# Head loads in modulation row pieces, three K blocks with their own history, and a new order of all engines, in a fused adaLN block on one Trainium2 core

## The chip, the core and the metric

The kernel runs on one core of a Trainium2 chip. The core has five instruction streams that run side by side and wait for each other through semaphores: TensorE (PE, matmuls), VectorE (DVE), ScalarE (ACT), GpSimd (POOL) and SyncE (SP, which here only issues DMAs). The metric is the device time of one execution in microseconds (us). All matrices are bf16.

## What is computed

One transformer block with modulation from a condition vector, for 2048 rows of 512 numbers. Cut to what matters:

```python
sa, ca, ga, sb, cb, gb = (silu(c) @ w_mod).reshape(6, 512)      # c: 1 x 512, w_mod: 512 x 3072
h = layernorm(x) * (1 + ca) + sa
q, k, v = h @ wqkv                                              # 32 heads of 16
# row s attends to the 8 rows s, s-2, ..., s-14 (rows before 0 are masked)
logits = einsum(q[s], k[s - 2w]) / 4;  attn = softmax(logits over w);  o = sum(attn * v[s - 2w])
x = x + ga * (o @ wo)
h = layernorm(x) * (1 + cb) + sb
x = x + gb * ((gelu(h @ w_gate) * (h @ w_up)) @ w_down)         # inner width 1792
```

## The kernel before, in words

**Groups.** The 2048 rows are worked in four groups of 512 (`sg` 0 to 3). A group goes through the first norm, its transposition to `hT` (columns on partitions), the projections to Q, K and V, the window attention, the output projection, the second norm and the feed-forward part. The four groups overlap: while one is in its feed-forward matmuls, the next ones are in attention.

**Attention.** Q, K and V lie transposed, in four column blocks `j`. For each block DVE multiplies Q with eight shifted views of K (`pq`, line 664, 128 x 4096 numbers), and PE sums the products over the 16 numbers of a head with a matrix of ones (`LTp`, line 678; small tiles, four side by side). After the softmax (mask, maximum, subtraction, exp, sum, reciprocal, probabilities: lines 690 to 722) DVE multiplies the probabilities with shifted copies of V (`pv`, line 771), and PE sums these over the window (`o_ps`, line 790). V's shifted copies come through memory: `vT` is stored (line 635) and loaded four times with different offsets into one tile `V` (line 644), each piece some 510 KB.

**K and its history.** `kT` (line 170) holds 16 columns and then three blocks of 512. Group `sg` writes block `sg % 3`, and its eight views reach back into the block before it, so a product of group 1 also waits for group 0's K. Group 3 takes block 0 again; one copy (`halo`, line 630) brings the last 16 columns of group 2 to the front for it.

**The head.** Group 0 is loaded in two halves of two 128-row chunks. Columns 0 to 1023 of `w_mod` (shift `sa` and scale `ca`) come as two DMAs of 512 columns each (`ldwm01`, line 242). PE multiplies each with silu(c): 16 small matmuls for one half (line 348), 16 for the other; DVE adds them up into `mod01` (line 355). Until there is work, PE runs 20 filler matmuls (`warmup`, line 217). Group 0's chunks are transposed on PE, two at a time (`th0`, `th1`; line 509), and evicted with scale and shift to `hT` by ACT (line 545) and DVE (line 543). The first two Q blocks are projected in halves of 256 rows as these come in (line 580), all else in 512 rows (line 598).

**The order.** Every step is an `Op` of a generator, with its engine; the list `ORDER` names, step by step, which generator goes on. So each engine's instruction order is fixed by hand, and an instruction that waits holds up all behind it on its engine. The names used below are those of the steps: `pq.1.3` is the product of group 1, block 3; `lp.1` group 1's last logits matmuls; `qp.1.0.2` the projection of group 1, Q (0; K is 1, V is 2), block 2; `pv.0.0` the first PV product and `o.0.2` the matmuls on the third; `mp2` to `mp5` the products for the other four modulation vectors, whose loads are `wm2` to `wm5`.

**Buffers.** PSUM is shared out as four banks `mm` (projections, feed-forward, modulation), two `att` (transposes, PV sums, output projection) and one tile `lg` of two banks for the logits. A matmul that needs a bank waits for the eviction of the one before in it. All big loads go through SP's queue, in the order of the list.

**The steps named in the prediction.** Normalisation: statistics on DVE (lines 430, 431) or ACT (408 to 419), reciprocal root on POOL (471), application on DVE (448). Groups 2 and 3 are transposed by a DMA (line 490); group 2's scale and shift is then done on POOL (line 525), group 3's on ACT (line 527).

Of the kernel before, what the change touches and what calls it, by code (L numbers as in the profile page):

```python
# [9 lines left out]
ALU = mybir.AluOpType  # L10
# [44 lines left out]
]  # L55


def _ap(base, free_dims):
    return bass.AP(base.tensor, base.offset, [list(base.ap[0])] + [list(d) for d in free_dims])


class Slots:


# [913 lines left out]
```

## Time and profile before

| what | value |
|---|---|
| time of three runs | 236.69 us median (236.52 to 236.73) |
| profiled execution: its span, from the first to the last instruction | 234.1 us |
| median of the runs less that span | 2.6 us |
| PE busy | 230.0 us, 98% of the span |
| DVE, ACT, POOL busy | 170.4, 150.0, 18.6 us |
| bytes moved | 30.21 MB, mean 129 GB/s |
| granted TensorE clock | 1.000 (mean of the span) |

The profiled execution's own time is known as its span; the runs are timed around it. A row of the timeline gives the start, the length, the engine, the line, the operation, what it writes and reads, and how many were merged into it. PEld is the loading of weights ahead of a matmul. A DMA row of SP is the issue alone; its landing is given in a view of its own, in us from the issue. The chain of work follows the end of the kernel back, from each step to what released it. In the view by stretch, an engine's busy time stands beside the length of the stretch.

### The profile page before, as it was taken

How to read it: one execution, taken by the hardware profiler on the slowest of the kernel's cores; microseconds unless marked ns; L12 is line 12 of the kernel's file. 1: busy time of each engine (PE TensorE's matmuls, PEld its weight loads, DVE VectorE, ACT ScalarE, POOL GpSimd, SP SyncE). 2: the span in 40 equal slices, each digit the busy share in tenths (PEclk: the TensorE clock that was granted, in tenths of full speed). 3: DMA queues.
4: the chain of work that ended last, by engine and by line, in shares of the span. 5: the costliest groups of instructions: out<-in, count | busy, mean ns of one | idle time of the engine just before them, and what ended most of it. 6: DMA issues, size and time to landing. Idle time of an engine off the chain costs nothing.

```text
span 234.1 us, 3675 instructions
## 1 busy us (share of the span) xinstructions
PE 230.0 (98%) x1387; PEld 108.2 (46%) x1387; DVE 170.4 (73%) x240; ACT 150.0 (64%) x283; POOL 18.6 (8%) x43
## 2 busy tenths in 40 slices
PE   7999999999999999999999999999999999999995
PEld 2755455434644444444444444444444444444443
DVE  3999999999997999999799788467747421222222
ACT  4899997976997758936656492546754343666400
POOL 2612461000100000100000010000001000000000
PEclk9999999999999999999999999999999999999999
DMA  6997989999969839553102963510000411000011
GB/s 218 373 364 213 202 213 171 276 391 303 176 152 236 291 92 200 98 114 103 56 0 57 202 109 60 156 56 0 0 4 0 90 45 45 3 0 0 0 48 45
DMA packets 36265, 30.21 MB, mean 129 GB/s; under 512 B 14872, under 2 KB 34328, under 8 KB 36248
## 3 DMA queue, kind: packets, MB, share of 16 engines
q1 hardware_dynamic: 35968, 29.72, 50.6%
q10 hardware_dynamic: 280, 0.26, 0.3%
q8 instruction: 11, 0.18, 0.3%
q14 instruction: 6, 0.05, 0.1%
HBM read 22.37 MB, written 4.98 MB: 117 GB/s over the span
## 4 chain that ended last, share of the span: by engine, by line
PE 98%; DVE 0%; issue 0%
PE g_ps L844 21%; PE u_ps L844 21%; PE y_ps L856 19%; PE qkv_ps L598 17%; PE x_ps L811 6%; PE o_ps L790 3%; PE LTp L678 3%; PE warm_ps L217 3%; PE y_ps L868 1%; PE qkv_ps L580 1%; PE hTp L484 1%; PE hTp L509 0%; PE modT_ps L305 0%; PE modT_ps L348 0%; PE gR_ps L369 0%; PE PTp L736 0%
## 5 line engine op out<-in xcount | busy, mean ns | idle before, releaser
L844 PE MATMUL g_ps<-h,Wg 128*128 128x512 bf16 x224 | 57.5, 379 | 0.0
L844 PE MATMUL u_ps<-h,Wu 128*128 128x512 bf16 x224 | 57.5, 379 | 0.0
L878 ACT ACTIVATE gl<-g_ps 128x512 bf16<-128x512 f32 x56 | 33.6, 600 | 24.8 <-PE g_ps L844 23.9
L856 PE MATMUL y_ps<-Wd,hht 128*128 128x512 bf16 x210 | 46.0, 379 | 0.0
L885 ACT CAST ub<-u_ps 128x512 bf16<-128x512 f32 x56 | 32.8, 586 | 18.3 <-PE u_ps L844 18.1
L598 PE MATMUL qkv_ps<-hT,wqkv 128*128 128x512 bf16 x184 | 42.1, 380 | 0.0
L896 DVE TENSOR_TENSOR hht<-gl,ub 128x512 bf16<-128x512 bf16 x56 | 23.0, 421 | 25.3 <-ACT ub L885 25.0
L664 DVE TENSOR_TENSOR pq<-qT,kT 128x4096 bf16<-128x4096 bf16 x16 | 36.3, 2292 | 0.0
L771 DVE TENSOR_TENSOR pv<-PT,V 128x4096 bf16<-128x4096 bf16 x16 | 36.0, 2286 | 0.0
L844 PEld LDWEIGHTS <-Wg 128*128 128x128 bf16 x224 | 21.5, 98 | 27.3 <-issue 2.1
L844 PEld LDWEIGHTS <-Wu 128*128 128x128 bf16 x224 | 21.8, 98 | 26.6 <-issue 0.4
L856 PEld LDWEIGHTS <-hht 128*128 128x128 bf16 x210 | 20.5, 98 | 24.8
L598 PEld LDWEIGHTS <-wqkv 128*128 128x128 bf16 x184 | 20.1, 114 | 19.7 <-issue 3.0
L903 DVE TENSOR_TENSOR ot<-y_ps,x 128x512 bf16<-128x512 f32 x15 | 10.3, 689 | 20.2 <-PE y_ps L856 17.2
L471 POOL TENSOR_TENSOR rstd<-rstd,neghalf 128x4 f32<-128x4 f32 (+1 forms) x9 | 8.8, 980 | 154.1 <-DVE rstd L460 85.5
L527 ACT ACTIVATE h<-h,modT,scl 128x512 bf16<-128x512 bf16 x12 | 8.8, 802 | 11.6 <-DMA h<-xn 11.6
L811 PE MATMUL x_ps<-woP,oT 128*128 128x512 bf16 x64 | 15.3, 379 | 0.0
L430 DVE BATCH_NORM_STATS2 st<-x 128x6 f32<-128x512 bf16 x19 | 12.9, 680 | 3.1 <-DMA x<-in_A_x_dram 2.9
L820 DVE TENSOR_TENSOR x<-x_ps,x 128x512 bf16<-128x512 f32 x16 | 10.8, 686 | 5.0 <-PE x_ps L811 5.0
L801 ACT CAST oT<-o_ps 128x512 bf16<-128x512 f32 x16 | 8.9, 592 | 2.7 <-PE o_ps L790 2.7
L618 ACT CAST qT<-qkv_ps 128x512 bf16<-128x512 f32 x16 | 9.2, 587 | 2.2 <-PE qkv_ps L598 2.1
L620 ACT CAST kT<-qkv_ps 128x512 bf16<-128x512 f32 x16 | 9.5, 596 | 1.2 <-PE qkv_ps L598 1.2
(85 smaller groups left out, 181.5 us busy)
## 6 DMA issues: line engine op xcount, KB each, us to landing
V<-vscr SPq DMA_DIRECT2D x12, 520.0 KB, 10.4
wm<-in_w_mod_dram SPq DMA_DIRECT2D x6, 512.0 KB, 5.4
vscr<-vT SPq DMA_DIRECT2D x4, 512.0 KB, 4.2
out_dram<-ot SPq DMA_DIRECT2D x15, 128.0 KB, 1.7
Wg<-in_B_w_gate_dram SPq DMA_DIRECT2D x1, 1792.0 KB, 11.0
Wu<-in_B_w_up_dram SPq DMA_DIRECT2D x1, 1792.0 KB
wqkv<-in_A_wqkv_dram SPq DMA_DIRECT2D x3, 512.0 KB, 8.3
x<-in_A_x_dram SPq DMA_DIRECT2D x3, 512.0 KB, 8.6
```

The source lines that it names most:

```text
L430: nc.vector.bn_stats(out=st[:], in_=src()[:, c4, :])
L598: nc.tensor.matmul(ps[:], lhsT=wqkv[blk][:, dt, j::4], rhs=B["hT", sg][:, :, dt, :], start=(dt == 0), stop=(dt == DT - 1))
L664: nc.vector.tensor_tensor(out=pq[:], in0=_ap(B["qT", sg][:, j, :], [[0, W], [1, SG]]), in1=_ap(kT[:, j, sg % 3 * SG + 2:sg % 3 * SG + 2 + ...
L771: nc.vector.tensor_tensor(out=t[:], in0=_ap(B["PT", sg][:, 0, :], [[SG, 2], [0, 4], [1, SG]]), in1=_ap(v[:, 0, j, :], [[8, 2], [4 * (SG + ...
L811: nc.tensor.matmul(ps[:], lhsT=B["oT", sg][:, j, c4::CPS] if sg else B["oT", sg][:, j, c4 * P:(c4 + 1) * P], rhs=woP[:, j, :], start=(j == ...
L820: nc.vector.tensor_tensor(out=x[:, c4, :], in0=B["x1ps", sg, c4][:], in1=x[:, c4, :], op=ALU.add)
L844: nc.tensor.matmul(ps[:], lhsT=Wt[:, dt, ft * P:(ft + 1) * P], rhs=B["h2T", sg][:, :, dt, :], start=(dt == 0), stop=(dt == DT - 1))
L856: nc.tensor.matmul(ps[:], lhsT=B["hh", sg, ft][:, c4 * P:(c4 + 1) * P], rhs=B["Wd", ft // 4][:, ft % 4, :], start=(ft == 0), stop=(ft == F ...
L878: nc.scalar.activation(out=gl[:], in_=B["g", sg, ft][:], func=ACT.Gelu_apprx_tanh)
L885: nc.scalar.copy(out=ub[:], in_=B["u", sg, ft][:])
L896: nc.vector.tensor_tensor(out=hh[:], in0=B["gl", sg, ft][:], in1=B["ub", sg, ft][:], op=ALU.mult)
L903: nc.vector.tensor_tensor(out=ot[:], in0=B["y", sg, c4][:], in1=B["x", sg][:, c4, :], op=ALU.add)
```

## The change

1. Columns 0 to 1023 of `w_mod` are loaded as four pieces of 128 rows (all 1024 columns, 256 KB each) instead of two halves of 512 columns. Each piece's eight products are issued as it lands, all four accumulating into one PSUM tile.
2. Wq is loaded as two DMAs of two row tiles each, and x of group 1 directly after it; both belong to the same SP sequence now.
3. 16 filler matmuls instead of 20.
4. Group 0 is transposed chunk by chunk (`th0` to `th3`), into other PSUM tiles: the first half into two `att` banks, the second into the `lg` tile and one `mm` bank. DVE evicts column tiles 0 and 2 of the first half and 0, 1, 2 of the second, ACT the rest. Three Q blocks instead of two are projected in halves.
5. `kT` becomes three blocks, each with its own 16 history columns; ACT copies the history for groups 1, 2 and 3 (`kh`) instead of for group 3 alone. A product no longer waits for the K block of the group before, but for that copy.
6. The mask lies, in bf16, in the third K block, until group 2 writes it; group 2's first K copy waits for the mask's use.
7. A new `ORDER` for all engines. What the steps below use of it: `mod01` now stands ahead of the last two chunks' normalisation on DVE; `pq.0.0` stands behind group 1's normalisation, and `pq.0.0` and `pq.0.1` both ahead of the last three chunks of group 2's, whose transposing DMA is issued on SP ahead of V's four pieces; group 3's normalisation stands behind the softmax's last two operations; `wm4` is loaded behind V's last piece, `wm5` ahead of group 0's V, and `gB` behind group 2's V store; `mp4` and `mp5` stand ahead of `lp.1` on PE, one V projection of group 3 behind it; the small-tile matmuls are grouped into 13 visits instead of 15.

```diff
 ORDER = [
-    23, 23, 23, 23, 23, 23, 23, 23, 23, 23, 23, 2, 0, 0, 23, 1, 1, 22, 2, 31, 31, 31, 33, 22, 23, 22, 33, 33,
...
+    2, 21, 21, 21, 21, 21, 21, 21, 21, 21, 0, 21, 0, 1, 1, 20, 2, 2, 2, 2, 2, 2, 2, 28, 28, 20, 20, 21, 28, 30,
...
 ]
-    maskT = const.tile([H, W, 16], F32, name="maskT")
-    kT = const.tile([P, 4, 3 * SG + 16], BF16, name="kT")
+    kT = const.tile([P, 4, 3, SG + 16], BF16, name="kT")
+    maskT = kT[0:H, 0, 2, 16:16 + 16 * W].rearrange("p (w s) -> p w s", s=16)
-        def ldwm01(b):
-            if "wm01" not in B:
-                B["wm01"] = T("prod", [P, 2, 4, D], BF16, "wm01")
-            nc.sync.dma_start(out=B["wm01"][:, b, :, :], in_=w_mod[:, b * D:(b + 1) * D].rearrange("(t p) n -> p t n", p=P))
+        def ldwm01(kt):
+            if kt == 0:
+                B["wm01"] = T("prod", [P, 4, 2 * D], BF16, "wm01")
+            nc.sync.dma_start(out=B["wm01"][:, kt, :], in_=w_mod[kt * P:(kt + 1) * P, 0:2 * D])
...
-            for b in (1, 0):
-                yield Op("SP", 0.5, lambda b=b: ldwm01(b), take=[SL["prod"]] if b else [], fire=f"wm{b}", lat=mb(0.5))
+            for kt in range(4):
+                yield Op("SP", 0.5, lambda kt=kt: ldwm01(kt), take=[] if kt else [SL["prod"]], fire=f"wm01.{kt}", lat=0.68)
+            for a in range(2):
+                yield Op("SP", 0.5, ld(wqkv[0][:, 2 * a:2 * a + 2, :], wq_v[:, 2 * a:2 * a + 2, 0:D]), fire=f"wqkv0.{a}", lat=0.72)
+            yield Op("SP", 0.55, ldx(1), fire="x1", lat=mb(0.5))
...
+        for kt in range(4):
+            def f(kt=kt):
+                if kt == 0:
                     B["mp01"] = T("mm", [P, 8], F32, "modT_ps")
+                for ch in range(8):
+                    nc.tensor.matmul(B["mp01"][:, ch:ch + 1], lhsT=B["wm01"][:, kt, ch * P:(ch + 1) * P],
+                                     rhs=scT[:, kt:kt + 1], start=(kt == 0 and ch == 0), stop=(kt == 3 and ch == 7))
...
+    ONV = {(0, True): (0, 2), (0, False): (1, 3), (1, True): (0, 1, 2), (1, False): (3,)}
+    def transp0(key, ev):
+        for c4 in range(CPS):
+            half, c = c4 // 2, c4 % 2
...
+    def qkv_halves():
+        def mm(half, j, dt, n):
+            nc.tensor.matmul(B["qkvps", 0, 0, j][:, half * 256:half * 256 + 256], lhsT=wqkv[0][:, dt, j::4],
+                             rhs=B["hT", 0][:, 2 * half:2 * half + 2, dt, :], start=(n == 0), stop=(n == DT - 1))
+        for dt in range(DT):
+            def f(dt=dt):
+                for j in range(3):
...
-    def halo():
-        yield Op("ACT", 0.25, lambda: nc.scalar.copy(out=kT[:, :, 0:16], in_=kT[:, :, 3 * SG:3 * SG + 16]),
-                 after=[f"qkv.2.1.{j}" for j in range(4)] + [f"pq.0.{j}" for j in range(4)], fire="halo")
+    def khalo(sg):
+        if sg:
+            yield Op("ACT", 0.25, lambda: nc.scalar.copy(out=kT[:, :, sg % 3, 0:16], in_=kT[:, :, (sg - 1) % 3, SG:SG + 16]),
+                     after=[f"qkv.{sg - 1}.1.{j}" for j in range(4)] + [f"pq.0.{j}" for j in range(4) if sg == 3], fire=f"kh.{sg}")
...
-                                        in1=_ap(kT[:, j, sg % 3 * SG + 2:sg % 3 * SG + 2 + SG], [[2, W], [1, SG]]), op=ALU.mult)
+                                        in1=_ap(kT[:, j, sg % 3, 2:2 + SG], [[2, W], [1, SG]]), op=ALU.mult)
...
-    pl.spawn(warmup(13, 20))
+    pl.spawn(warmup(13, 16))
```

The numbers `w` and `lat` of an `Op` are notes of the list's author and have no effect on the kernel.

More of the change, by code (lines that the diff above doesn't have):

```diff
@@ L200, in f2 @@
         def f2():
[L201 removed]
+            nc.gpsimd.memset(kT[:, :, 0, 0:16], 0.0)
             nc.gpsimd.memset(M2[:], 0.0)
@@ L545, in f @@
                         nc.scalar.activation(out=o, in_=i, func=ACT.Identity, scale=sc(dt), bias=bi(dt))
-                yield Op("DVE" if onv else "ACT", 0.32 if onv else 0.455, f, after=[f"{ev}.th{half}"] + dep,
-                         take=[SL["hT"]] if dt == 0 and half == 0 else [], give=[SL["mm" if half else "att"]] if n == len(dts) - 1 else [],
-                         fire=f"{ev}.h{dt}.{half}")
+                give = [] if dt != ONV[half, eng][-1] else [SL["att"]] if half == 0 else [SL["lg" if eng else "mm"]]
+                yield Op("DVE" if eng else "ACT", 0.32 if eng else 0.455, f, after=[f"{ev}.th{2 * half + 1}"] + dep,
+                         take=[SL["hT"]] if dt == 0 and half == 0 else [], give=give, fire=f"{ev}.h{dt}.{half}")
     stat = pool("stat_p", 4)
@@ L570, with f @@
     QKV = [(0, 0), (1, 0), (2, 0), (2, 1), (2, 2), (2, 3), (0, 1), (1, 1), (0, 2), (1, 2), (0, 3), (1, 3)]
-    QKV0 = [(0, 0), (0, 1), (0, 2), (1, 0), (1, 1), (0, 3), (1, 2), (2, 0), (2, 1), (2, 2), (2, 3), (1, 3)]
+    QKV0 = [(0, 0), (0, 1), (0, 2), (0, 3), (1, 0), (1, 1), (1, 2), (2, 0), (2, 1), (2, 2), (2, 3), (1, 3)]
     def qkv_halves():
-        for half in range(2):
-            for n, dt in enumerate(((2, 0, 3, 1), (0, 1, 2, 3))[half]):
-                def f(half=half, n=n, dt=dt):
-                    for j in range(2):
-                        if half == 0 and n == 0:
-                            B["qkvps", 0, 0, j] = T("mm", [P, SG], F32, "qkv_ps")
-                        nc.tensor.matmul(B["qkvps", 0, 0, j][:, half * 256:half * 256 + 256],
-                                         lhsT=wqkv[0][:, dt, j::4], rhs=B["hT", 0][:, 2 * half:2 * half + 2, dt, :],
-                                         start=(n == 0), stop=(n == DT - 1))
-                yield Op("PE", 0.218, f, after=[f"LN1.0.h{dt}.{half}", "wqkv0"],
-                         take=[SL["mm"]] * 2 + [SL["q"]] if half == 0 and n == 0 else [], fire=f"qph.{half}.{dt}")
-        for j in range(2):
-            pl.done[f"qp.0.0.{j}"] = pl.done["qph.1.3"]
+        def mm(half, j, dt, n):
[4 more added lines that the diff above has]
+                for j in range(3):
+                    if dt == 0:
+                        B["qkvps", 0, 0, j] = T("mm", [P, SG], F32, "qkv_ps")
+                    mm(0, j, dt, dt)
+            yield Op("PE", 0.328, f, after=[f"LN1.0.h{dt}.0", f"wqkv0.{dt // 2}"],
+                     take=[SL["mm"]] * 3 + [SL["q"]] if dt == 0 else [], fire=f"qph.{dt}")
+        for j in range(3):
+            def f(j=j):
+                for dt in range(DT):
+                    mm(1, j, dt, dt)
+            yield Op("PE", 0.437, f, after=[f"LN1.0.h{dt}.1" for dt in range(DT)], fire=f"qp.0.0.{j}")
     def qkv(sg):
@@ L601, in qkv @@
             tk = {0: [SL["q"]], 1: [], 2: [SL["vs"]]}[blk] if j == 0 else []
-            yield Op("PE", 0.856, f, after=[f"LN1.{sg}.h{d}" for d in (("0.1", "1.0", "3.1") if sg == 0 else (2, 3))] + [f"wqkv{blk}"], take=[SL["mm"]] + tk,
+            yield Op("PE", 0.856, f, after=[f"LN1.{sg}.h{d}" for d in (("2.1", "3.1") if sg == 0 else (2, 3))] + ([f"wqkv{blk}"] if blk else []), take=[SL["mm"]] + tk,
                      give=[SL["hT"]] if last else [], fire=f"qp.{sg}.{blk}.{j}")
@@ L619, in g @@
                 elif blk == 1:
-                    nc.scalar.copy(out=in_rows(kT[:, j, 16 + sg % 3 * SG:16 + (sg % 3 + 1) * SG], sg), in_=by_rows(ps, sg))
+                    nc.scalar.copy(out=in_rows(kT[:, j, sg % 3, 16:16 + SG], sg), in_=by_rows(ps, sg))
                 else:
```

74 lines of the change are left out of this document (32 added, 42 removed), and 68 rows, old and new, of the table ORDER.

## The prediction

> **What bounds the kernel now.** I read the page first, then the chain of work in order of time, then busy time by stretch, then the timeline. The page gives the span:
>
> ```profile
> span 234.1 us, 3675 instructions
> ```
>
> The chain (start, length, what) stays on TensorE (PE) from 1.25 to 231.30 without a gap, so the end moves by what is taken off PE's stream, plus any wait that the new order puts into it:
>
> ```profile
> 1.20 0.05 issue
> 1.25 4.88 PE warm_ps L217 x11
> ...
> 8.98 0.45 PE hTp L509 x8
> 9.43 0.65 PE warm_ps L217 x3
> 10.07 1.85 PE qkv_ps L580 x16
> ...
> 54.19 0.55 PE LTp L678 x8
> ...
> 92.24 1.84 PE LTp L678 x32
> 94.08 0.97 PE g_ps L844 x4
> 95.05 0.86 PE u_ps L844 x4
> ...
> 120.63 1.29 PE LTp L678 x24
> ...
> 231.30 0.02 issue
> ```
>
> Busy time by stretch shows a second engine that is full. Its columns are length, PE, PEld, DVE, ACT, POOL, clock, DMA share, GB/s:
>
> ```profile
> 10.07:54.12 44.05, 44.05 (x325) 22.28 (x322) 43.60 (x51) 38.44 (x84) 9.61 (x8) 1.00 1.01 271
> ```
>
> From 10.07 to 54.12 VectorE (DVE) works 43.60 of 44.05 us, at the granted clock of 1.00, and the DMA engines are full too (share 1.01). PE's matmuls on pq and pv take what DVE makes. A shorter PE stream is worth something only if DVE is earlier as well. The place where the two meet is lp.1 (LTp at 54.19), group 1's last logits, which needs the product pq.1.3:
>
> ```profile
> 41.68 4.49 DVE L771 TENSOR_TENSOR pv<-PT,V 128x4096 bf16<-128x4096 bf16 x2
> ...
> 51.63 2.29 DVE L664 TENSOR_TENSOR pq<-qT,kT 128x4096 bf16<-128x4096 bf16 x1
> ```
>
> It ends at 53.92, and PE reaches lp.1 at 54.19: 0.27 us of margin.
>
> **PE's own sum.** Twenty fillers become sixteen, and the transposes go chunk by chunk. The head's timeline before:
>
> ```profile
> 8.01 0.41 DVE L448 TENSOR_SCALAR xn<-x,mv,rstd 128x512 bf16<-128x512 bf16 x1 [0.27 <-POOL rstd L471]
> 8.34 0.41 DVE L448 TENSOR_SCALAR xn<-x,sums,rstd 128x512 bf16<-128x512 bf16 x1
> 8.78 0.17 DVE L355 TENSOR_TENSOR mod<-modT_ps,c 128x8 f32<-128x8 f32 x1
> 8.98 1.68 DVE L543 TENSOR_SCALAR hT<-hTp,mod 128x256 bf16<-128x256 bf16 x5
> 10.58 0.69 DVE L430 BATCH_NORM_STATS2 st<-x 128x6 f32<-128x512 bf16 x1
> ```
>
> The last normalised chunk is done at 8.75. Four transposes end by 9.10 (8 take 0.45), two fillers at 0.65/3 end at 9.53, and the first projection starts there instead of at 10.07: **-0.54**. Its operand is ready: mod01 moves into the 0.27 us idle before 8.01, the first hT pass starts near 8.76 instead of 8.98 and ends at 9.17. A third block in halves costs 8 x 0.116 (1.85/16) for one 0.86: **+0.06**. Each visit of the small-tile matmuls costs a switch: 32 take 1.84, where 24 take 1.29 (0.43 per 8), so 0.12 going in, and the next group takes 0.97 for 0.86, 0.11 going out. The lists have 15 visits before and 13 after: **-0.45**, half of it ahead of lp.1. PE alone: -0.93.
>
> Ahead of lp.1 PE also gains mp4 (0.38) and mp5 (0.22) and loses one projection (0.86), which pass lp.1 in the other direction. PE could be there at 54.19 - 0.54 + 0.06 - 0.22 + 0.60 - 0.86 = 53.23, and has then 0.04 more left to do than before.
>
> **DVE's sum.** Both lists give DVE the same operations up to pq.1.3; only their order differs. It starts its first group-1 statistic after the five hT passes: 8.76 + 1.68 = 10.44, with the same overlap of the next start some 10.40 instead of 10.58, so **-0.18**. That needs x1 by then. Landings are known here (issue in the timeline, landing in us after it):
>
> ```profile
> 1.31 1.00 SPq L245 DMA_DIRECT2D wm<-in_w_mod_dram  x2
> 2.36 0.51 SPq L223 DMA_DIRECT2D wqkv<-in_A_wqkv_dram  x1
> 3.48 0.44 SPq L223 DMA_DIRECT2D wqkv<-in_A_wqkv_dram  x1
> ```
>
> ```profile
> wm<-in_w_mod_dram SPq DMA_DIRECT2D x1, 512.0 KB, 4.6
> wqkv<-in_A_wqkv_dram SPq DMA_DIRECT2D x1, 512.0 KB, 6.6
> wqkv<-in_A_wqkv_dram SPq DMA_DIRECT2D x1, 512.0 KB, 8.3
> ```
>
> So 5.91, 8.96 and 11.78, with one 512 KB load between each two: some 1.45 us for each, the loads queue behind each other. The second half of wm lands near 7.43 (bounds 5.91 and 8.96), x1 near 10.37. The order of these bytes is kept, so the fourth piece lands near 7.43 too, its products end near 7.65, and mod01 fits.
>
> Were the load of V in time, pq.1.3 would end at 53.74 and lp.1 start 0.05 later (DVE to PE in the row at 1.20), at 53.79: 0.40 earlier than before, 0.36 with the 0.04, 236.3.
>
> **The load of V.** The new DVE order puts a second 2.2 us product ahead of the last group-2 normalisations, whose transposing DMA stands on SP ahead of all of V's pieces:
>
> ```profile
> 20.56 0.41 DVE L448 TENSOR_SCALAR xn<-x,sums,rstd 128x512 bf16<-128x512 bf16 x1
> 20.88 8.89 DVE L664 TENSOR_TENSOR pq<-qT,kT 128x4096 bf16<-128x4096 bf16 x4
> ```
>
> ```profile
> 21.09 3.42 SPq L490 DMA_TRANSPOSE hT<-xn  x1
> 24.61 0.62 SPq L644 DMA_DIRECT2D V<-vscr  x1
> ...
> 31.54 1.72 SPq L644 DMA_DIRECT2D V<-vscr  x2
> ```
>
> ```profile
> V<-vscr SPq DMA_DIRECT2D x1, 506.0 KB, 9.2
> ```
>
> The normalisation ends at 20.97 + 2.22 - 0.18 = 23.0, so the transposing DMA and V's first piece are issued 1.9 us later. The last piece (506 KB) is issued near 32.3 and lands near 41.5; DVE takes it up at 41.68. Three things give back: the DMA engines were partly idle in three stretches of 1 us, together 1.0 us, and the load of gB (128 KB in SBUF, some 0.35 us at the 512 KB per 1.45 us of above) now goes behind V:
>
> ```profile
> 26.00:27.00 1.00, 1.00 (x6) 0.54 (x5) 1.00 (x1) 1.00 (x4) 0.38 (x1) 1.00 0.68 120
> ...
> 31.00:32.00 1.00, 1.00 (x6) 0.56 (x5) 0.97 (x2) 1.00 (x4) 1.00 (x3) 1.00 0.66 125
> 32.00:33.00 1.00, 1.00 (x7) 0.48 (x6) 1.00 (x2) 1.00 (x5) 0.67 (x1) 1.00 0.67 197
> ```
>
> Ends: 0 (all absorbed) and +1.9. I take 1.9 - 1.0 - 0.35 = 0.55, so V is whole at 42.05, where DVE stands ready at 41.50. pv.0.0 starts 0.37 later than before, pq.1.3 ends at 54.29, lp.1 starts at 54.34: +0.15, and 0.04 behind it: **+0.19**. PE waits 1.1 us in all for DVE ahead of lp.1, and that wait eats the head's gain.
>
> **What this wait hides.** Every other new wait ahead of lp.1 costs nothing up to 1.1 us in sum. The rows for the three that I found:
>
> ```profile
> 10.54 0.63 ACT L408 ACTIVATE gl<-x 128x512 bf16<-128x512 bf16 x1
> 12.25 1.54 ACT L618 CAST qT<-qkv_ps 128x512 bf16<-128x512 f32 x3
> ...
> 36.01 1.38 DVE L448 TENSOR_SCALAR xn<-x,sums,rstd 128x512 bf16<-128x512 bf16 x4
> ```
>
> ```profile
> L527 ACT ACTIVATE hT<-hT,mod 128x512 bf16<-128x512 bf16 x4 | 3.0, 809 | 0.0
> ```
>
> At the first K projection (qp.0.1.0) four PSUM banks are full and the first Q copy must free one. ACT's statistics of x1 take from 10.4 on what they took before (12.25 - 10.54 = 1.7), a sum for x2 follows (0.6), the copy (some 0.55) ends near 13.3; PE is there at 9.53 + 24 x 0.116 + 0.86 = 13.17. wm4, now loaded behind V's last piece, lands near 42.05 + 1.45 = 43.5; mp4 stands 9.9 us of PE work ahead of lp.1, so PE wants it at 53.23 - 9.9 = 43.3. Group 3's normalisation has the softmax's last two operations ahead of it (2.0 us) and ends at 37.39 + 2.0 - 0.18 = 39.2; its transposing DMA takes 5.5 (21.09 to the start of GpSimd's passes at 26.6, below), four ACT passes 3.0, so to 47.7, and behind them on ACT wait the output copies: the bank that o.0.2 takes is free near 48.3. pv.0.2, which o.0.2 needs as well, ends at 42.05 + 3 x 2.25 = 48.8, later. Without the cover these three would cost PE 0.2 to 0.6 us. The two added history copies lie in ACT's 5.6 idle us of that stretch, and the copy that now waits for the mask's use (done near 30) comes after 36 anyway. Behind lp.1 the running sums leave DVE over 1 us ahead of PE, but for o.1.3 and o.2.3, where it is about 0: 0 to +0.3, taken as 0.
>
> Group 2's hT passes on GpSimd now start near 23.0 + 5.5 = 28.5. Before, one took five times as long as the others:
>
> ```profile
> L525 POOL TENSOR_SCALAR hT<-hT,mod x4: 767/768/3802, 26.6 to 31.9; 128x512 bf16<-128x512 bf16 x4
> ```
>
> The long one lay beside DVE products and ended when DVE read PSUM. That stretch stays near 29.7 to 32.4, so they end near 32.7, and PE, 24.8 us of stream after 9.53, needs them from 34.3. The Trainium skill, SBUF — State Buffer, "Who interferes with whom", says that a DVE operation with both inputs in SBUF holds GpSimd's reads out wholly; the trace agrees with 3.80 against 0.77 us. Without that lock, four passes at the mean 1.53 would end near 34.6 and just touch PE.
>
> **Rivals.** (1) Slower: V's pieces keep the full 1.9 us, because the three idle stretches come from SP's waits, which move along. Then pv.0.0 starts at 43.4, lp.1 at 55.69: +1.54, 238.2. It decides as soon as pv.0.0 starts after 41.86. For it: the DMA share of 1.01 over the whole stretch. Against: the idle time in them. (2) Faster: DVE doesn't bind, PE's sum stands: 236.69 - 0.93 = 235.8. Against it: 43.60 of 44.05. (3) The change doesn't bring the head forward: three more DMAs, at 0.5 us of SP issue each, push x1 back 1.5 us, to 11.9, and DVE with it: lp.1 at 53.92 + 1.3 + 0.05 = 55.27, 237.8. Against it: the loads queue at 1.45 us each, behind which the issue hides. The Trainium skill, DMA: Bandwidth & Descriptors, "Bandwidth", tells to batch to 1 MiB or more and so speaks for this rival; the 512 KB loads above ran at 360 KB per us all the same.
>
> **How the numbers follow.** The sum is made against the profiled span, 234.1 to 234.3; the runs' median, 236.69, lies 2.6 us above the span, and I let that stand: 236.9. Chances: forecast 0.40 (own range 236.3 to 237.3), (1) 0.34, (2) 0.15, (3) 0.11. A measurement of this kernel tells about 0.2% (0.47 us) from no change. Faster by more: 0.17, the second rival and the forecast's low end. Slower by more: (1), most of (3) and the forecast's high end, 0.45. Within: 0.38. The range runs from (2) to (1): 235.7 to 238.3.
>
> **What would show it.** Right: the first projection halves at 9.5; 0.2 to 1.5 us of PE idle between 13 and 54, most of it before PV or logits matmuls, released by DVE; DVE idle before the first pv, released by V's DMA; lp.1 near 54.3; no PE idle behind. Wrong: lp.1 before 53.5 (DVE found time), pv.0.0 at 41.5 with lp.1 late all the same (another wait decides), or PE idle behind 54.

## The result and the profile after

The changed kernel takes 238.97 us (median of six runs, 238.54 to 239.50), the kernel before on the same chip 236.77 (six runs, 236.52 to 237.68). The ratio is 1.0082, 95% interval 1.0066 to 1.0099: **slower by 2.2 us**, outside the forecast of 236.9 and 0.7 above the end of its range. The profiled execution took 239.14. The page of after, with the granted clock in 40 slices and the chain:

```profile
span 236.9 us, 3670 instructions
...
PEclk9799999999999999999999999999999999999999
...
PE 84%; DVE 7%; DMA 3%; ACT 2%; issue 2%; SPq 1%; DVEq 0%
...
L673 DVE TENSOR_TENSOR pq<-qT,kT 128x4096 bf16<-128x4096 bf16 x16 | 36.2, 2291 | 1.6 <-ACT kT L639 1.6
```

Before, the chain lay on PE throughout; now 16% of it lies elsewhere. Two things on this page belong to the change: a slice near the start in which the clock fell, and 1.6 us in which the products wait for line 639, the new history copy. The meeting point of PE and DVE, lp.1, stands at 54.12 in PE's timeline before (54.19 in the chain) and at 56.74 after:

```profile
54.12 0.61 PE L678 MATMUL LTp<-pq,Mph 128*32 128x512 bf16 x8
```

```profile
56.74 0.61 PE L687 MATMUL LTp<-pq,Mph 128*32 128x512 bf16 x8
```

That is +2.62 of the span's +2.8; behind lp.1 it is 180.16 against 179.98 us. The loss sits ahead of lp.1. DVE's timeline (the bracket is the idle time before, and what ended it) gives its parts:

```profile
8.37 0.17 DVE L356 TENSOR_TENSOR mod<-modT_ps,c 128x8 f32<-128x8 f32 x1 [0.75 <-PE modT_ps L350]
...
9.89 0.73 DVE L548 TENSOR_SCALAR hT<-hTp,mod 128x256 bf16<-128x256 bf16 x2 [0.71 <-PE hTp L515]
...
11.82 0.69 DVE L431 BATCH_NORM_STATS2 st<-x 128x6 f32<-128x512 bf16 x1
...
25.82 6.70 DVE L673 TENSOR_TENSOR pq<-qT,kT 128x4096 bf16<-128x4096 bf16 x3 [1.61 <-ACT kT L639]
...
44.34 8.89 DVE L780 TENSOR_TENSOR pv<-PT,V 128x4096 bf16<-128x4096 bf16 x4
```

The first group-1 statistic starts 1.24 us later than before (11.82 against 10.58), and pq.0.2 waits 1.61. Together 2.85; pv.0.0 is 2.66 later (44.34 against 41.68). DVE reaches it without a pause, so in this execution it does not wait for V's load. Why the head is late, PE's timeline shows:

```profile
6.58 0.35 PE L350 MATMUL modT_ps<-scT,wm 128*128 128x1 bf16 x8 [0.56 <-DMA wm<-in_w_mod_dram]
7.32 0.36 PE L350 MATMUL modT_ps<-scT,wm 128*128 128x1 bf16 x8 [0.39 <-DMA wm<-in_w_mod_dram]
7.97 0.37 PE L350 MATMUL modT_ps<-scT,wm 128*128 128x1 bf16 x8 [0.28 <-DMA wm<-in_w_mod_dram]
8.20 1.01 PE L217 MATMUL warm_ps<-gB 128*128 128x512 bf16 x2
9.00 1.91 PE L515 MATMUL hTp<-ident,xn 128*128 128x128 bf16 x16
...
11.21 2.78 PE L580 MATMUL qkv_ps<-hT,wqkv 128*128 128x256 bf16 x24
```

The fourth piece's products start at 7.97, not near 7.43; two fillers and 16 transposes take 1.01 and 1.91 us, where the layout run below, with the same head at full clock, has 0.59 and 1.05; the first projection starts at 11.21 here, 11.38 in the chain, instead of at 9.53. By stretch (length, PE, PEld, DVE, ACT, POOL, granted clock, DMA share, GB/s):

```profile
6.00:7.00 1.00, 0.37 (x9) 0.27 (x8) 0.93 (x5) 0.98 (x3) 0.72 (x1) 1.00 1.03 360
7.00:8.00 1.00, 0.39 (x9) 0.32 (x10) 0.63 (x2) 0.93 (x2) 0.94 (x3) 0.72 1.03 363
8.00:9.00 1.00, 1.00 (x10) 0.45 (x11) 0.63 (x3) 0.00 (x0) 0.72 (x5) 0.50 1.08 373
...
11.00:54.00 43.00, 41.52 (x345) 22.27 (x344) 41.01 (x50) 38.04 (x85) 8.43 (x7) 1.00 0.96 240
```

Waiting for pieces, PE is busy 0.37 and 0.39 of two microseconds; inside the second of them the clock falls (0.72 on average), and it is 0.50 until shortly before 11, so that fillers and transposes take nearly twice as long. From 11 to 54 DVE works 41.01 of 43.00 us where it had been full.

### The profile page after: what moved, and what is told of

Same layout as the page of the kernel before. It is cut to its first block, busy times and chain, and to the rows that moved or that the text cites. A ratio compares the mean times of both kernels' runs of the same rounds, so it can differ in the third digit from the quotient of the medians.

```text
span 236.9 us, 3670 instructions
## 1 busy us (share of the span) xinstructions
PE 229.4 (97%) x1376; PEld 109.8 (46%) x1387; DVE 169.4 (72%) x240; ACT 150.3 (63%) x285; POOL 17.8 (8%) x43
## 4 chain that ended last, share of the span: by engine, by line
PE 84%; DVE 7%; DMA 3%; ACT 2%; issue 2%; SPq 1%; DVEq 0%
PE g_ps L853 21%; PE u_ps L853 20%; PE y_ps L865 19%; PE qkv_ps L607 8%; PE x_ps L820 6%; DVE pq L673 3%; PE o_ps L799 3%; DMA wm<-in_w_mod_dram 2%; PE LTp L687 2%; PE y_ps L877 1%; DMA woP<-in_A_wo_dram 1%; PE qkv_ps L580 1%; DVE pv L780 1%; ACT hT L533 1%; PE hTp L515 1%
## 5 line engine op out<-in xcount | busy, mean ns | idle before, releaser
L905 DVE TENSOR_TENSOR hht<-gl,ub 128x512 bf16<-128x512 bf16 x56 | 22.7, 419 | 29.2 <-ACT ub L894 29.1
L607 PE MATMUL qkv_ps<-hT,wqkv 128*128 128x512 bf16 x180 | 40.8, 380 | 0.0
L853 PEld LDWEIGHTS <-Wu 128*128 128x128 bf16 x224 | 21.8, 98 | 26.7 <-issue 0.4
L409 ACT ACTIVATE gl<-x 128x512 bf16<-128x512 bf16 x13 | 8.2, 635 | 3.5 <-DVE x L829 3.5
L633 ACT CAST vT<-qkv_ps 128x512 bf16<-128x512 f32 x16 | 9.1, 588 | 1.9 <-PE qkv_ps L607 1.8
```

What stands on the lines that cost most here:

```text
L607: nc.tensor.matmul(ps[:], lhsT=wqkv[blk][:, dt, j::4], rhs=B["hT", sg][:, :, dt, :], start=(dt == 0), stop=(dt == DT - 1))
L853: nc.tensor.matmul(ps[:], lhsT=Wt[:, dt, ft * P:(ft + 1) * P], rhs=B["h2T", sg][:, :, dt, :], start=(dt == 0), stop=(dt == DT - 1))
L905: nc.vector.tensor_tensor(out=hh[:], in0=B["gl", sg, ft][:], in1=B["ub", sg, ft][:], op=ALU.mult)
```

## The experiments

Theory **A** says that the history copies aren't free. `kh` writes 16 columns in each of four column blocks of one tile; in the layout [column block][K block] the stretch from its first to its last address spans K block 0 of the later column blocks, so pq.0.2, which stands behind it in the list and needs nothing of it, waits. Theory **B**: the head's pieces come too late for their place, PE idles and the clock falls. Theory **C**: the order of the loads costs time, since K's and V's weights now stand behind x2 (x of group 2; x1 is that of group 1). Rival **D**: V's load comes too late, rival 1 of the prediction. An "x to y" beside a ratio is its 95% interval; times are medians, beside the kernel before on the same chip, and a range of times is that of the runs.

**A, by layout.** The same copies, but the K block outside the column block:

```diff
-    kT = const.tile([P, 4, 3, SG + 16], BF16, name="kT")
+    kT = const.tile([P, 3, 4, SG + 16], BF16, name="kT")
-  kT[:, j, sg % 3, ...]   kT[:, :, sg % 3, 0:16]
+  kT[:, sg % 3, j, ...]   kT[:, sg % 3, :, 0:16]
```

> The changed kernel with the K tile laid out block by block (three blocks outside, the four column blocks inside) instead of column block by column block; the same numbers, instructions and order. Theory (overlap in layout): VectorE's 1.61 us wait at 25.82 is not needed by any number. It stands before pq.0.2, a product of group 0, which reads nothing of group 1's history copy; but in the old layout the history's 4 x 16 columns span all column blocks in memory, pq.0.2's K lies inside that span, and it waits for the copy. With the blocks outside, the span is block 1 alone: pq.0.2 starts at 24.2, lp.1 near 55.3 instead of 56.81, time 237.4 to 237.6 (238.97 less 1.4 to 1.6). Rival (the copy is late and truly needed, ScalarE's lateness is the cause): the wait stays at pq.0.2 or moves whole to the next product, no gain, 238.9. Second rival (the load of V decides the first pv): pv.0.0 stays past 43.8, gain under 0.5, 238.5 or more.

238.15 (before 236.80), ratio 1.0058 (1.0037 to 1.0078). DVE's timeline of this kernel:

```profile
10.78 0.68 DVE L431 BATCH_NORM_STATS2 st<-x 128x6 f32<-128x512 bf16 x1
...
23.09 6.68 DVE L673 TENSOR_TENSOR pq<-qT,kT 128x4096 bf16<-128x4096 bf16 x3
...
33.00 2.51 DVE L673 TENSOR_TENSOR pq<-qT,kT 128x4096 bf16<-128x4096 bf16 x1 [0.49 <-ACT kT L629]
...
42.88 2.29 DVE L780 TENSOR_TENSOR pv<-PT,V 128x4096 bf16<-128x4096 bf16 x1 [0.51 <-ACT vT L633]
```

The wait at pq.0.2 is gone with nothing but the layout changed, and 0.82 us of time with it (237.76 to 238.59 against 238.54 to 239.50). Two later waits take the rest: pq.1.1 for its K (0.49), and pv.0.0 (0.51). The second is put down to a vT copy, but of the two copies that can be meant one was done 1 us earlier (41.84), and the other still runs at pv.0.0's start in the third kernel of "Everything mended" (from 42.23 on, against 42.42). So V's load is what is left. A is shown; D sits right behind it. The first row tells of the head: this execution has the same head with the clock at 1.00, and its first statistic stands at 10.78, so of the 1.24 us of the profile after, 1.04 came with the fall.

**A, by order.** The copy for group 1 goes ahead of ACT's first two sums of group 3:

```diff
 ACT, behind the fourth K copy of group 0:
-  sums of group 3 (two chunks), kh.1
+  kh.1, sums of group 3 (two chunks)
```

> The changed kernel, old layout, with group 1's history copy ahead of ScalarE's first two statistics of group 3 (1.24 us) instead of behind them; nothing else. Theory (overlap): pq.0.2 still waits for the copy, which now starts as soon as the last K copy of group 0 is done at 24.35, so pq.0.2 starts near 24.6 instead of 25.82: time 237.7 to 237.9, a little less gain than with the other layout. If the history copy isn't what decides: 238.9.

238.59 (before 236.80), 1.0072 (1.0053 to 1.0091): 0.4 less in the median, though the runs touch those of the changed kernel (238.05 to 238.74 against 238.54 to 239.50). DVE still waits 2.41 us in this profile, because the last K copy was late too: K's and V's weights came late there (V's at 18.0), and PE waited 0.73 and 1.04 for them. Moving the copy forward doesn't take the wait away; the layout does.

**B.** Five more fillers, two, two and one ahead of the pieces 2, 3 and 4, on the changed kernel and together with the layout:

```diff
 PE:
-  12 fillers, mp01.0, mp01.1, mp01.2, mp01.3, fillers, transposes
+  12 fillers, mp01.0, 2 fillers, mp01.1, 2 fillers, mp01.2, 1 filler, mp01.3, fillers, transposes
```

> The changed kernel with five filler matmuls more, two ahead of the second piece's products, two ahead of the third's, one ahead of the fourth's, so that TensorE isn't idle while it waits for the pieces. Theory (clock): the granted clock stays at 1.00 from 7.4 to 10.9, where it was 0.50 in the profiled run; the fillers and transposes behind the products take half the time, the first projection starts near 9.7 instead of 11.38, group 1's first statistics near 10.8 instead of 11.82, time 0.5 to 1.0 less: 238.0 to 238.5. Since three of the six runs of the changed kernel show a mean clock of 1.000 and are 0.5 us faster in the mean than the others, the gain of the median is the smaller end. Rival (the pieces land late, the order of the head is the cause, not the clock): the clock stays or not, but the first projection stays past 10.8 and the time at 238.9.

> Both edits: K blocks outside and five more fillers. If the two causes are separate and all that VectorE lost, the gains add: 238.97 - 1.5 - 0.6 = 236.9, lp.1 near 54.5 in the profile. If the load of V takes over once VectorE is earlier (pv.0.0 held by V's pieces), the sum is not reached: 237.3 or more, with VectorE idle just ahead of pv.0.0.

Fillers alone: 239.03, 1.0096 (1.0076 to 1.0116), no gain. Fillers and layout: 237.69, 1.0042 (1.0023 to 1.0060), 0.46 less than the layout alone, which is not clear of noise (237.52 to 238.19 against 237.76 to 238.59). The first projection starts at 10.31 and 9.85. In the second, DVE's first statistic is no earlier than in the layout's profile: it waits 0.22 us for x1 and starts at 10.96. Why the fillers do nothing by themselves shows one row of DVE's timeline of the first:

```profile
25.75 2.29 DVE L673 TENSOR_TENSOR pq<-qT,kT 128x4096 bf16<-128x4096 bf16 x1 [2.19 <-ACT kT L639]
```

An earlier DVE waits longer for the same copy: 2.19 instead of 1.61. So in the changed kernel A covers whatever B is worth. The granted clock stayed at 0.998 or above in all 60 runs of kernels with these fillers; without them 10 of 22 runs of kernels with the new head had a mean of 0.992 or 0.993. In the changed kernel itself the two groups of runs lie 239.1 and 239.5 against 238.5 to 239.1, and in the layout kernel there is no difference (238.0 and 238.3 against 237.8 and 238.6). So the fall costs at most some 0.5 us: part of it is hidden as well.

**Pieces without the rest.** The kernel before with change 1 alone (four row pieces, products piece by piece; nothing else moved):

```diff
-            for b in (1, 0):
-                yield Op("SP", ..., ldwm01(b), ...)
+            for kt in range(4):
+                yield Op("SP", ..., ldwm01(kt), ...)
 PE:
-  mp01 of one half, mp01 of the other
+  mp01.0, mp01.1, mp01.2, mp01.3
```

> The kernel before with the head's loads of the changed one alone: four DMAs of 128 rows instead of two of 512 columns, each piece's eight products in its turn (two pieces where one half stood), 20 fillers and all else as before. By the prediction's third rival (three more issues of 0.5 us push x of group 1 back) VectorE starts its statistics at 11 or later and the time is 237.2 or more; if the loads queue behind each other and the issue hides, x lands as before and the time is 236.7 to 236.9. No clock fall is expected, since fillers run until the products.

236.66 (12 runs; before 236.83, 19 runs), ratio 0.9997 (0.9986 to 1.0009): no difference. Its first statistic stands at 10.84, the clock holds. Rival 3 put x1 at 11.9; two of its three added DMAs cost no time here, and in three kernels that have all three DVE waits for x1 until 10.96, 11.15 and 11.34 (0.22, 0.32 and 0.47 us), not 11.9. mod01 ahead of the last two normalisations waits 0.50 to 1.10 us in the profiles of the new head; what its place alone costs, no run shows.

**C.** wqkv1 ahead of x2 and wqkv2 ahead of wo1 and wo2 in the changed kernel; the reverse in the kernel before:

```diff
 SP in the changed kernel:
-  x1, x2, wqkv1, wo1, wo2, wqkv2
+  x1, wqkv1, x2, wqkv2, wo1, wo2
 SP in the kernel before:
-  x1, wqkv1, x2, wqkv2, ...
+  x1, x2, wqkv1, wo1, wo2, wqkv2, ...
```

> The changed kernel with two loads moved in the list of SyncE's queue: K's weights ahead of x of group 2, V's weights ahead of the first two pieces of Wo (the order of the kernel before); nothing else. Theory: three of the four runs so far show TensorE waiting 0.5 to 1.0 us for these weights at the first K projection (14.1 to 14.6, the weights landing 14.0 to 14.6, against 11.8 before), and this lateness runs through the K copies to group 1's history copy, for which VectorE waits. With K's weights 1.4 us earlier that wait on TensorE goes, but the first Q copies end near 13.5 and hold the PSUM banks, so 0.5 to 0.9 us remain as gain of the history copy: time 238.1 to 238.5. If the weights' order costs nothing (ScalarE or the clock decides): 238.9.

> The kernel before with only the loads' order of the changed one: x of group 2 ahead of K's weights, two pieces of Wo ahead of V's weights. If the order of these loads is a cause by itself, TensorE waits about 0.5 us at its first K projection, and VectorE, which is full, can't give it back: 236.8 + 0.3 to 0.6 = 237.1 to 237.4. If it is hidden (VectorE needs the first K block only at 14.86): 236.8.

In the kernel before, the load order alone costs 1.5 us: 238.23 (before 236.74), 1.0068 (1.0049 to 1.0086), and PE shows where:

```profile
14.52 7.10 PE L598 MATMUL qkv_ps<-hT,wqkv 128*128 128x512 bf16 x32 [1.67 <-DMA wqkv<-in_A_wqkv_dram]
```

Undoing it in the changed kernel gains nothing: 239.20, 1.0107 (1.0087 to 1.0127). ACT's timeline of that kernel, and PE's row behind it:

```profile
13.67 0.63 ACT L409 ACTIVATE gl<-x 128x512 bf16<-128x512 bf16 x1 [0.99 <-DMA x<-in_A_x_dram]
14.20 0.19 ACT L409 ACTIVATION_READ_ACCUMULATOR gl<-x 128x1 f32 x1
14.30 1.54 ACT L627 CAST qT<-qkv_ps 128x512 bf16<-128x512 f32 x3
```

```profile
14.91 1.46 PE L607 MATMUL qkv_ps<-hT,wqkv 128*128 128x512 bf16 x6 [1.40 <-ACT qT L627]
```

The new ACT order has a sum over x2 ahead of the Q copies that free PSUM. With x2 later, the sum waits, the copies behind it wait, PE waits. The load order and the ACT order have to fit each other; the next kernels mend them together.

**Everything mended, step by step.** Layout, fillers and loads (first); then group 2's last three normalisations ahead of pq.0.1, so that its transposing DMA can be issued earlier (second); then the sum over x2 behind the first three Q copies (third):

```diff
 DVE (second):
-  one chunk of group 2, pq.0.1, three chunks
+  four chunks of group 2, pq.0.1
 ACT (third):
-  sum over x2, Q copies 0 to 2
+  Q copies 0 to 2, sum over x2
```

> K blocks outside, five more fillers and the two loads moved, together. Theory: in the run with the first two, VectorE idled 0.29 us at pq.1.1 for a K copy, and V was whole only about when VectorE came to it (pv.0.0 at 42.72, straight behind pq.1.2). Earlier weights bring the K and V copies, and with them V's store (22.34) and load, 0.5 us forward, pq.1.1 loses its wait: 237.69 - 0.3 to 0.5 = 237.2 to 237.4. Rival: x of group 2 now lands later and VectorE waits for its statistics instead, or x of group 1 (10.7 to 10.95) still decides: 237.6 to 237.8.

> As the last, and group 2's last three normalised chunks ahead of the second product of group 0 on VectorE, so that their transposing DMA and V's pieces behind it in SyncE's queue don't wait for a 2.2 us product. By the prediction's first rival (V's pieces late by that product), V lands up to 1 us earlier and pv.0.0 follows VectorE alone: 0.2 to 0.4 less than the last run. If V's own store (issued after the V copies, 22.3, and landing 4.3 us later) decides the first V piece and not the transposing DMA: no difference within 0.1.

> As the run with all three edits and group 2's normalised chunks moved, and ScalarE's first sum over x of group 2 put behind the first three Q copies instead of ahead of them. Theory: in the three runs with K's weights ahead of x of group 2 ScalarE idles 0.94 to 0.99 us for that x, ahead of the Q copies, and TensorE 1.4 to 1.56 us for the PSUM bank that the first copy frees: the load order and ScalarE's order have to fit each other. With the sum behind the copies the first K projection starts near 13.5 instead of 15.0, pq.1.1's wait of 0.50 for a K copy goes, V's store and load come 1 us earlier: 238.09 - 0.5 to 0.8 = 237.3 to 237.6. If VectorE's late start (group 1's statistics at 10.95 to 11.15, x of group 1 landing then) is all that is left, no more than 0.5 is to be had; if V's load or the bank isn't what decided, no gain: 238.0.

238.21, 1.0061 (1.0041 to 1.0080); 238.09, 1.0061 (1.0037 to 1.0086); 237.70, 1.0041 (1.0026 to 1.0056, eight runs). The first two have ACT's wait for x2 (0.94 us in the first); the third has neither that nor a wait for weights, and still only equals layout and fillers. The second tells something of D: with the normalisation out of the way (done at 21.8), SP issues the transposing DMA at 24.30 all the same. What SP waits for there is group 0's store of vT (22.90, with a load of Wo behind it), not the normalisation that my prediction named.

**Misses on the head.** mod01 behind the last two normalisations again, with further small moves (first: group 2's variance step behind group 1's normalisation as well; second: on top of the V edit below):

```diff
 DVE:
-  mod01, chunks 2 and 3 of group 0
+  chunks 2 and 3 of group 0, mod01
 SP:
-  wqkv0.0, wqkv0.1, x1
+  wqkv0.0, x1, wqkv0.1
 PE (second only):
-  two fillers, th0, th1
+  th0, th1, two fillers
```

> As the last, and three edits to the head's order: mod01 behind group 0's last two normalised chunks on VectorE again (as before the change), the last statistic of group 2 behind group 1's normalisation (it waits 0.38 us for ScalarE), x of group 1 loaded ahead of the second half of Q's weights. Theory: VectorE starts group 1's statistics near 10.6 instead of 10.95, and loses 0.38 less behind them: 0.4 to 0.7 less than the last, 236.7 to 237.0, level with the kernel before. Rival: the half of Q's weights that comes later holds the first projection and ScalarE with it, no gain.

> As the last, with the head's order mended: mod01 behind group 0's last two normalised chunks on VectorE, the first two chunks' transposes ahead of two of the fillers on TensorE, x of group 1 loaded ahead of the second half of Q's weights. Theory (VectorE is full from its first statistic of group 1 on, and starts it at 10.75 to 11.03 where the kernel before has 10.58): that statistic starts near 10.6, 0.3 to 0.4 less than the last, 236.8 to 237.0, level with before. Rival: the later half of Q's weights, or mod01's later place, costs as much as x's landing gains: 237.2 or more.

238.50, 1.0074 (1.0059 to 1.0089), and 239.34, 1.0107 (1.0090 to 1.0125). In the first, hT waited 0.62 us for transposes that stood behind fillers, and the moved variance step made DVE wait 0.90 for GpSimd's root: my own move. The second had hT at 8.92 and statistics at 10.82, nearer to the forecast head, and gained nothing on the 239.14 of its parent, in which another wait decides (below).

**What is left: V.** Every mended kernel so far ends at 237.7 or above, with pv.0.0 between 42.4 and 43.4 (41.68 before). The products of mp3 were moved behind group 1's K, which takes pq.1.1's wait away:

```diff
 PE and ACT:
-  mp3, mod3, qp.1.1.0, qp.1.1.1
+  qp.1.1.0, qp.1.1.1, mp3, mod3
```

> As the run with ScalarE's sum behind the Q copies, and the products mp3 (0.49 us of TensorE with the switch between tile sizes) moved from ahead of group 1's projections to behind the projection whose K copy pq.1.1 waits for. Theory (what is left is TensorE's order ahead of group 1's second K block and second V store): that copy ends 0.49 us earlier, pq.1.1's wait of 0.50 goes, V's second store and last pieces are issued 0.4 us earlier, pv.0.0 starts near 41.9 instead of 42.42: 237.7 - 0.4 to 0.5 = 237.2 to 237.3. If V's pieces are held by something else (transfer, not store), pv.0.0 stays at 42.4 and the gain is under 0.2.

237.76, 1.0046 (1.0031 to 1.0060): that wait is gone, pv.0.0 waits 0.53 at 42.74 instead. Then V's third and fourth piece were issued ahead of group 1's store of vT, behind which they wait on SP, in three kernels (the last one, the layout kernel, the kernel before):

```diff
 SP:
-  V piece 0, 1, store of vT (group 1), V piece 2, 3
+  V piece 0, 1, 2, 3, store of vT (group 1)
```

> As the run with mp3 moved, and the third and fourth piece of group 0's V issued directly behind the second, ahead of group 1's V store; in the list that store, which waits until 31.7 for group 1's V copies, stands between them on SyncE's queue and needs nothing of them. Theory (V's load is what is left): V is whole near 37, VectorE's idle time of 0.53 ahead of pv.0.0 goes, pv.0.0 starts straight behind pq.1.2 near 42.1: 237.76 - 0.5 = 237.2 to 237.3. If pv.0.0 waits for something else (the transposed probabilities' copies, 41.6): no gain, 237.7.

> The changed kernel with only two edits: K blocks outside, and V's third and fourth piece ahead of group 1's V store. With the K blocks alone VectorE idled 0.51 us ahead of pv.0.0 (42.88). If V's load is that wait: 238.15 - 0.5 = 237.6 to 237.7. If not: 238.1.

> The kernel before with V's third and fourth piece of group 0 issued directly behind the second, ahead of the load of gB and group 1's V store. In its profile V was taken up at 41.68 straight behind the product before it, without idle time, so VectorE bound there: 236.7, no difference; in executions in which V lands a little later (0.42 us idle in the run with the row pieces) it gains, so at most 0.2 to 0.3 in the median: 236.5.

239.14 (1.0096, 1.0080 to 1.0112), 239.95 (1.0128, 1.0111 to 1.0145) and 240.67 (1.0153, 1.0126 to 1.0180): all slower, in the kernel before as well. ACT's timeline of the first:

```profile
42.28 1.07 ACT L633 CAST vT<-qkv_ps 128x512 bf16<-128x512 f32 x2 [3.28 <-DMA vscr<-vT]
43.24 1.09 ACT L754 CAST PT<-PTp 128x512 bf16<-128x512 f32 x2
```

There is one vT buffer. The store, issued at 32.04 behind 1 MB of V, landed some 10 us later, and the next group's V copies waited for it. Behind them on ACT stand the copies of the transposed probabilities (`PT`), for which DVE then waits 1.81 us at pv.0.0. V itself is no longer late: its last piece is issued at 29.2 and lands 11.4 us later, at 40.6, ahead of DVE. So the edit takes V's lateness away, with group 0's store of vT no earlier than in the other mended kernels (22.13), and puts a dearer wait in its place. The next edit brings group 1's store forward instead, by taking two of ACT's sums from ahead of the V copies:

```diff
 ACT:
-  two sums of squares of group 3, V copies 2 and 3 of group 1
+  V copy 2, sum, V copy 3, sum
```

> As the run with mp3 moved, and on ScalarE two sums of squares of group 3 (0.8 us each) behind the V copies of group 1 that they stood ahead of. Theory (V's load is what is left, held on SyncE's queue by group 1's V store): that store is issued at 31.2 instead of 31.7, V's last two pieces follow it, V is whole 0.5 us earlier, the idle 0.53 us ahead of pv.0.0 go, and pv.0.0 starts near 42.2: 237.76 - 0.4 to 0.5 = 237.3. If V's transfer and not its issue decides: under 0.2 gained.

> As the last, with the three edits of the head's order (mod01 behind group 0's last chunks, two transposes ahead of two fillers, x of group 1 ahead of the second half of Q's weights). Its DVE part was seen to start group 1's statistics at 10.82 instead of 11.03. Theory: VectorE gains 0.2 more, pv.0.0 near 42.0: 237.1. If V's load is again the later of the two: no gain over the last, 237.3.

238.06 (1.0050, 1.0031 to 1.0069) and, with the head edits, 237.83 (1.0044, 1.0027 to 1.0060): both missed. The first one's issues on SP, and its pv.0.0:

```profile
22.01 0.65 SPq L644 DMA_DIRECT2D vscr<-vT  x1
...
26.88 1.38 SPq L653 DMA_DIRECT2D V<-vscr  x2
31.10 0.56 SPq L644 DMA_DIRECT2D vscr<-vT  x1
31.71 1.71 SPq L653 DMA_DIRECT2D V<-vscr  x2
```

```profile
42.67 8.90 DVE L780 TENSOR_TENSOR pv<-PT,V 128x4096 bf16<-128x4096 bf16 x4 [0.67 <-ACT vT L633]
```

The last two pieces are issued about where they were before (31.71 against 31.54), and V is whole 1 us later all the same (by 41.68 at the latest before, near 42.67 here). What differs most is the start: the first store 1.7 us later (20.34 before), the first piece 2.3 later (24.61 before). One row by stretch of the kernel before, then of this one:

```profile
22.00:24.00 2.00, 2.00 (x26) 1.02 (x23) 2.00 (x2) 2.00 (x5) 0.00 (x0) 1.00 1.04 270
```

```profile
22.00:24.00 2.00, 1.63 (x20) 0.40 (x19) 2.00 (x2) 2.00 (x4) 0.00 (x0) 1.00 0.53 182
```

Before, the DMA engines are full in this stretch; here half of it is empty, and from 24 to 42 their share is 0.89 to 1.42 in each 2 us: V's work starts 2 us later, and there is little idle time left to catch up in. (From 20 to 22 it is the other way round, 0.25 before and 0.62 here, with other loads.) The first store is late because of PE's new order. PE before and in this kernel:

```profile
11.76 7.93 PE L598 MATMUL qkv_ps<-hT,wqkv 128*128 128x512 bf16 x36
19.53 0.61 PE L484 MATMUL hTp<-ident,xn 128*128 128x128 bf16 x8
```

```profile
17.99 0.61 PE L485 MATMUL hTp<-ident,xn 128*128 128x128 bf16 x8
18.95 0.41 PE L370 MATMUL gR_ps<-wm,scB 128*32 128x128 bf16 x16 [0.35 <-DMA wm<-in_w_mod_dram]
19.29 1.92 PE L607 MATMUL qkv_ps<-hT,wqkv 128*128 128x512 bf16 x8
```

Before, group 0's last V projection is done ahead of group 1's transposes; now transposes and the gate's products stand ahead of the last two V blocks (1.30 us from 17.99 to 19.29), and two hT evictions ahead of their copies on ACT. This chain, from PE's order by the first store to V, was read from the traces and not put to a run of its own, and three traces speak against the first store as the whole cause. V was whole at 40.6 with that store at 22.13, when the four pieces followed each other. And in the kernel before with pieces alone the store stands at 20.46, with the loads' order alone at 22.27, but V's last piece lands at 42.3 (33.3 and 9.0) and 42.6 (34.9 and 7.7). There the last piece is issued 1.1 and 2.7 us later than before (32.2), and that place, behind group 1's store, counts as well.

## Why the prediction was wrong

**"PE could be at lp.1 at 53.23", and the first projection at 9.53: wrong.** It started at 11.38. I let "the order of these bytes" stand for a landing at 7.43; the fourth piece's products began at 7.97, and the others came spread out, with PE idle between them. mod01 didn't fit into 0.27 us of idle time, it made one of 0.75. So DVE's term of -0.18 came out as +1.24: +0.20 in the layout run, which has the same head at full clock, and the rest with the fall. In the time the head is worth less: the fillers recover 0.46 us in the median once the next wait is out of the way, and that is not clear of noise. On what follows the idle time, the Trainium skill, TensorE: Matmul & The Clock Gate, "Part 1: The HAM clock gate", says that the array's clock has two states, half and full, and falls after a window of some 3.4 us without work. The 0.50 in the rows agrees with the first; the fall came within the second of two microseconds that were 0.37 and 0.39 busy, which is no idle window of that length. The Trainium skill, TensorE: Matmul & The Clock Gate, "A second HAM failure mode: psum-queue depth-cycling", tells of a kernel whose clock went to and fro from many short idle stretches; that is nearer to these rows. I had priced no fall at all.

**"The two added history copies lie in ACT's 5.6 idle us": the failing step.** I asked whether ACT had time for them, not who waits for them. A product that needs nothing of the copy waited 1.61 us for it, because the new layout makes the copy's stretch cover what the product reads. The layout run puts it at 0.82 us of time, the largest part of the 2.2 that one edit took back; the rest of the 1.61 was covered by the waits behind it.

**The order of the loads: left out.** I moved x1 and wm4 through SP's queue but not K's and V's weights, which went behind x2. By itself that is worth 1.5 us in the kernel before; in the changed kernel it lies under the other waits, and undone together with ACT's order it adds nothing to 237.7.

**"V whole at 42.05" and rival 1: right place, wrong cause.** With the false wait gone, pv.0.0 starts 0.7 to 1.8 us later than before, where I took 0.37 and rival 1 took 1.7, and in four of the mended kernels DVE waits there 0.5 to 0.9 us for V's load. But the step that I gave, the transposing DMA behind a second product, decides nothing (238.09 against 238.21). What moved V in the runs is the place of its last two pieces: ahead of group 1's store they have V whole at 40.6. What the late first store of vT adds stays open. In the changed kernel itself DVE comes later than V, so V costs nothing there.

**Right:** DVE and PE meet at lp.1 after as before (pq.1.3 ends at 56.56, lp.1 starts at 56.74), and an earlier PE by itself, with fillers alone, gains nothing; the hidden waits of mp4 and o.0.2 stayed hidden; behind lp.1 there is 0.18 us more, where I named 0 to 0.3.

**The sum of the runs.** Of 2.2 us, layout and fillers together take back 1.3: 0.8 is the false wait for the history copy, and 0.5 came off with the fillers, not clear of noise by itself. Some 0.9 remains in the best mended kernels (237.70 against 236.83, and 237.69 with layout and fillers alone). In the profile of the first of these, with a span 1.0 us longer than that of the kernel before, 0.7 lies ahead of lp.1: DVE's first statistic is 0.17 later, and pq.1.1 waits 0.50 for a K copy; V's load stands right behind, as the kernel shows in which mp3 was moved. 0.3 lies behind lp.1. Single profiles carry some noise: the spans of the kernel before run from 234.1 to 235.4, and pieces alone gave pv.0.0 at 42.51 in an execution of 236.98 us while its median was that of before. So the cause of the 0.9 stays open, and with it the share of PE's order ahead of the first store. No version here beats the kernel before clear of noise.

## What to carry to other kernels

When a copy or a write is added, ask who stands behind it in the list and touches any address between its first and its last, not only whether its engine has time; put the dimension that the writes go by outermost. An order for one engine rests on the landing order of the loads and on the order of the engine that frees its buffers, so undoing one of them alone can show nothing, and a wait that is taken away shows the next one. Where an engine waits for small pieces, look at the granted clock by stretch; here fillers between the pieces held it in all 60 runs, though the time that this saved is not clear of noise.

## What was not expected of the hardware

The granted TensorE clock fell to 0.50 for some 3 us in part of the executions of a kernel and not in others (10 of 22 with the new head), after scattered waits of 0.28 to 0.65 us. In both traces that have it the fall lasted 3.4 us, but began at different times: 7.4 to 10.8 in the changed kernel, 8.3 to 11.7 in the layout kernel with the V edit. In the 3.41 us ahead of it, as long a stretch, PE was busy for 2.38 and 2.17. That is no threshold: with the loads' order alone PE was busy for some 1.75 of the 3.41 us around its wait of 1.67, and the clock of that execution held. The new head isn't the only place for the fall: with the V edit, the kernel before had a mean clock of 0.993 in three of six executions too (240.75 to 241.10 against 239.15 to 240.59); where it fell there, its profile, taken at 1.000, can't show.

A DVE product of 128 x 4096 takes 2.28 us, but the one beside GpSimd's passes on hT took 2.51 us in the layout kernel and 2.81 with layout and fillers. The Trainium skill, SBUF — State Buffer, "Who interferes with whom", says that of two such operations the one issued first holds the shared ports for its whole length. The rows agree in kind: beside the 2.81 us product one GpSimd pass took 2.81 us instead of 0.77, and the product itself lost 0.53.

A 512 KB store landed in 4.2 and 5.2 us (medians of the kernel before and of the first kernel with the two sums moved), and in some 10 us behind two more loads of 0.5 MB.
